# Pooled attention with a top-1 mixture of experts: part of the routing moves from VectorE to GpSimd and ScalarE, three weight pieces are split later, the row scatters lose their fillers

## The chip, the core and the metric

The kernel runs on one core of one Trainium2 chip. The core has five engines with queues of their own: TensorE (PE in the profile, with its weight loads as PEld), VectorE (DVE), ScalarE (ACT), GpSimd (POOL) and SyncE (SP), which here only issues DMA transfers. Each engine works through its queue in order; an instruction that waits holds up all behind it. The metric is the device time of one execution in microseconds, less is better.

## The reference

```python
def _attn_ref(q, k, v):                      # (8, 8, 576, 64) each
    k_p = k.reshape(B, H, 72, 8, D).mean(axis=3)
    v_p = v.reshape(B, H, 72, 8, D).mean(axis=3)
    scores = scale * np.matmul(q, k_p.transpose(0, 1, 3, 2))
    scores = scores - np.max(scores, axis=-1, keepdims=True)
    attn = np.exp(scores)
    attn = attn / (np.sum(attn, axis=-1, keepdims=True) + 1e-09)
    return np.matmul(attn, v_p)

def _moe_ref(x, w_gate, w1, w2):             # x: 4608 tokens of 512; 8 experts, 512 -> 1024 -> 512
    logits = x @ w_gate
    expert_idx = np.argmax(logits, axis=1)
    probs = softmax(logits)                  # maximum taken off, 1e-9 added to the sum
    gate_w = probs[np.arange(N), expert_idx]
    for e in range(E):                       # the rows of each expert
        h = np.maximum(x_sorted[lo:hi] @ w1[e], 0.0)
        y_sorted[lo:hi] = h @ w2[e]
    return gate_w[:, None] * y
```

## The kernel before, in words

**Attention.** The 4608 tokens are cut into 36 units of 128 (i = 0 to 35 in the loop at line 968). A unit's steps run over the engines in a fixed order: TensorE turns the queries (g_qt) and forms the scores two units ahead (g_s), VectorE takes the minimum (g_min), ScalarE the exponentials (g_exp); TensorE turns the probabilities (u_pt), ScalarE and VectorE write them as a high and a low half (u_pt's activation, "ph", and u_lo, "pl", line 519), TensorE multiplies them with the values (u_pv, lines 540 and 545) into one single PSUM tile `po`, and VectorE normalises (u_nrm: lines 577, 579, 581, 586, 588). The next unit's u_pv waits until lines 581 and 586 have emptied `po`.

**Keys and values.** GpSimd adds up groups of eight keys and values of each batch (pool_k, pool_v: lines 322 to 325, three large additions each). TensorE, ScalarE and VectorE turn and split them (prep); the last step, `low` (line 420), is on GpSimd, and behind it SyncE issues some 13 small copies of each batch into the masked tile vb (line 1002, at most four for a unit, `moves`). u_pv of that batch's units needs these copies.

**Routing.** The units are grouped by 6, 6, 6, 6, 6, 4 and 2 (groups 0 to 6). When a group's logits are there, `route` hands over a chain of some 18 small steps: maximum (`top`, 622), subtraction (`away`, 625), the choice of the expert (`best`, 631, `lowest`, `onehot`, 646), counting, ranks, the softmax sum (`total`) with its `guard` (679), and `gate`. They go into a list, `fillers`, and the unit loop takes one at each of about six fixed places of a unit (`fill`). `off` is true for groups 0 to 4: their steps `before_all`, `ident_ids`, `carry` and `spot_int` run on GpSimd. Behind group 2, `early_pe` to `early_shift` (720) note whether expert 0 has its first 256 rows.

**Scatters.** A group's rows are sent to the expert's place in DRAM by one indirect DMA for each unit (`scatter`, line 694, issued by GpSimd). They stand in the list `pend`; `flush(1)` takes one at the start of each unit, and a second one in the middle while more than two wait (line 997). The rows lie in a ring of 12 slots (XR); u_nrm of a unit writes the slot that a unit twelve before it had. Between two scatters with no larger GpSimd work between them, `apart` (line 599) puts two memsets of 128x512 as fillers, up to unit 29.

**Weights of expert 0.** Eight pieces are loaded (wload, line 100) into staging tiles and written as a high half (ScalarE, line 114, hooks at units 12 to 28) and a low half: pieces 0, 2, 5, 6, 7 on GpSimd (lines 122 and 123, at units 14, 20, 31, 26, 30), pieces 1, 3 and 4 on VectorE in quarters (`lsplit`, line 856) from the units that line 862 names.

**Around unit 30.** Behind unit 28's GpSimd work the tile xg is blanked (blank_x); in unit 29 SyncE loads the first 256 rows of expert 0 into it (early_load, line 906). At the start of unit 30 GpSimd's queue holds, in this order, the low half of weight piece 7, `first_block` (line 882 and following: it splits the loaded rows, so it waits for that load), one scatter, and then the steps that the chain of group 4 puts on GpSimd.

**Experts.** Behind the attention a loop of some 22 blocks of 256 rows runs the two layers of the experts on TensorE (lines 956 to 958 and 1027).

The places that the change touches:

Of the kernel before, what the change touches and what calls it, by code (L numbers as in the profile page):

```python
# [12 lines left out]
AF = mybir.ActivationFunctionType  # L13
OP = mybir.AluOpType
# [4 lines left out]
SX = 2.0 ** 6  # L19
SW = 2.0 ** 5  # L20
# [12 lines left out]
def kernel(  # L33
# [10 lines left out]
    nc = tc.nc  # L44
    B, H, S, D = q.shape
    N, Dm = out.shape
    E = w1.shape[0]
# [54 lines left out]
    last_pool = []  # L102
# [63 lines left out]
    zpad = consts.tile([128, XW], F32, name="zpad")  # L166
# [18 lines left out]
    tv = consts.tile([128, 1], F32, name="tv")  # L185
# [5 lines left out]
    okf = consts.tile([128, 1], F32, name="okf")  # L191
# [97 lines left out]
    KVS = {}  # L289
# [8 lines left out]
    def fill_pe():  # L298
        if fillers and fillers[0][1]:
            fillers.pop(0)[2]()  # L300
# [155 lines left out]
    def g_qt(G, j):  # L456
        b, r = units[groups[G][0]]
        pq = psA.tile([128, 512], F32, name="pq", bufs=2)
        for x in range(4):
            if r is None:  # L460
                src = ql[(b // 2) % 2][:, 2 * x:2 * x + 2, :].rearrange("p h d -> p (h d)")
            else:
                src = qt[b % 2][:, 4 * j + x, r:r + 2, :].rearrange("p r d -> p (r d)")
            nc.tensor.transpose(pq[:, x * 128:(x + 1) * 128], src, ident)
        if j == 0:
            QT[G] = work.tile([128, 8, 128], F32, name="qT", bufs=2)
        nc.scalar.activation(QT[G][:, 4 * j:4 * j + 4, :].rearrange("p h t -> p (h t)"), pq, AF.Copy)
# [4 lines left out]
    def g_s(G, j):  # L472
        b, r = units[groups[G][0]]
        ps = psA.tile([128, 512], F32, name="ps", bufs=2)
        t = QT[G]
        if r is None:
            for x in range(2 * j, 2 * j + 2):
                for s in range(2):
                    bd = BD[(b + s) % 3].rearrange("p s h x -> p (s h) x")
                    rhs = bd[:, 2 * x:2 * x + H + 2:H + 1, :]  # L480
                    nc.tensor.matmul(ps[64 * s:64 * s + 64, (x % 2) * 2 * KP:(x % 2 + 1) * 2 * KP],
                                     t[:, x, 64 * s:64 * s + 64], rhs, start=True, stop=True)
            slots = [(4 * j + x, 0) for x in range(4)]
        else:
            hs = range(2 * j, 2 * j + 2)
            for x, h in enumerate(hs):
                nc.tensor.matmul(ps[:, x * 2 * KP:(x + 1) * 2 * KP], t[:, h, :],  # L487
                                 BD[b % 3][:, :, h, :], start=True, stop=True)
            slots = [(h, s) for h in hs for s in range(2)]
        PS_[G, j] = (ps, slots)  # L490
        if j == stages(G) - 1:
            QT.pop(G)
# [7 lines left out]
    def g_exp(G, j):  # L500
        ps, nmx, slots = PS_.pop((G, j))
        for x, (h, s) in enumerate(slots):
            p = pbuf[groups[G][s] % 4]
            nc.scalar.activation(p[:, h * KP:(h + 1) * KP], ps[:, x * KP:(x + 1) * KP], AF.Exp,  # L504
                                 bias=nmx[:, x:x + 1], scale=-1.0)

    def u_pt(i):
        p = pbuf[i % 4]
        pp = psA.tile([128, 1024], F32, name="pp")
        for c in range(5):  # L510
            nc.tensor.transpose(pp[:, c * 128:(c + 1) * 128], p[:, c * 128:(c + 1) * 128], ident)
        ph = work.tile([128, 640], F16, name="ph")
        nc.scalar.activation(ph, pp[:, 0:640], AF.Copy, scale=SP)
        PP_[i] = (pp, ph)
# [76 lines left out]
    pend = []  # L591

    def flush(n=99, upto=99):
        while n and pend and pend[0][0] <= upto:
            _, f, u = pend.pop(0)
            f(u)
            n -= 1

    def apart():
        if last_pool and not KVS.get("late"):  # L600
            nc.gpsimd.memset(zpad[:, 0:Dm], 0.0)
            nc.gpsimd.memset(zpad[:, 0:Dm], 0.0)
        last_pool[:] = [1]

    EARLY = 3
# [1 line left out]
    def route(gidx):  # L607
        i0, gs = bounds[gidx]
        X, L = GRP.pop(gidx)
        L = L[:, 0:gs, :]  # L610
        sh = [128, gs, E]
        V = nc.vector
        off = gidx < len(bounds) - 2
        Z = {}

        def new(n, shape, dt=F32):
            Z[n] = work.tile(shape, dt, name="r" + n)
            return Z[n]
# [3 lines left out]
            V.tensor_reduce(m[:, :, 0], L, axis=AX.X, op=OP.max)  # L622

        def away():
            V.tensor_tensor(new("a", [128, 6, E])[:, 0:gs], L, Z["m"][:, 0:gs].to_broadcast(sh), op=OP.subtract)

        def soft():
            nc.scalar.activation(new("ex", [128, 6, E])[:, 0:gs], Z["a"][:, 0:gs], AF.Exp, scale=1.0 / SX)
# [47 lines left out]

        def guard():
            es = Z["es"][:, 0:gs]
            V.tensor_scalar(es, es, 1e-9, SX * SW * SW, op0=OP.add, op1=OP.mult)

        def spot_int():
            p = new("pos", [128, 6], I32)[:, 0:gs]
# [34 lines left out]
            V.tensor_copy(oki, okf[0:1, :])  # L717

        def early_shift():
            V.tensor_tensor(tv, tv, okf, op=OP.add)  # L720

        if gidx == len(bounds) - 1:
            return [top, away, best, lowest, before_all, onehot, count, carry], rank, \
                [ranked, spot, spot_int, total, ident_ids, guard, gate], soft, scatters
        chain = [before_all, top, away, best, lowest, onehot, soft, ident_ids, count, rank, carry, total, ranked, spot,
                 spot_int, guard, gate, scatters]
        if gidx == EARLY - 1:
            chain += [before_all, early_pe, early_int, early_shift, lambda: KVS.update(early=1)]
        for f in chain:
# [74 lines left out]
    def put(i, pos, f, *a):  # L804
        assert 0 <= i < NU
        hooks.setdefault((i, pos), []).append((f, a))
# [52 lines left out]
        put(at, "act2", wsplit, 0, j, "h")  # L859
    for j, at, what in ((0, 14, 'P'), (2, 20, 'P'), (5, 31, 'p'), (6, 26, 'p'), (7, 30, 'p')):  # L860
        put(at, "q", wsplit, 0, j, what)
    for j, at in ((1, 15), (3, 23), (4, 26)):
        for x in range(4):
            put(at + x, "dve" if x % 2 else "dve2", lsplit, j, x, 4)

# [61 lines left out]
    def run(i, pos):  # L927
        for f, a in hooks.pop((i, pos), []):
            f(*a)
# [38 lines left out]
    for i in range(NU):  # L968
        A, Z = halves.get(2 * i), halves.get(2 * i + 1)
        Y = halves.get(2 * i - 1)  # L970
        run(i, "q")
        flush(1)
        if i:
            u_pt(i)
        if A:
            g_s(*A)
        if Y:
            g_exp(*Y)
        if i in turns:
            g_qt(*turns[i])  # L980
        if (i, "pe") not in hooks:
            fill_pe()
        run(i, "pe")
        if i:
            u_lo(i)
        fill()
        if A:
            g_min(*A)
            fill()
            g_exp(*A)  # L990
        run(i, "act")
        run(i, "dve")
        u_pv(i)
        run(i, "pe2")
        if i == 29:
            KVS["late"] = 1
        if len(pend) > 2:
            flush(1)
        fill_pe()
        run(i, "sp")  # L1000
        for _ in range(min(4 if i < 30 else 8, len(moves))):
            nc.sync.dma_start(*moves.pop(0))
        if Z:
            g_s(*Z)
        u_nrm(i, (lambda: g_min(*Z)) if Z else None)
        run(i, "act2")
        run(i, "dve2")
        last = routes(i)
        fill(2 if i >= NU - 3 else 1)
# [3 lines left out]
    front, rank, back, soft, scatters = last  # L1013
    V = nc.vector
# [288 lines left out]
```

## Time and profile before

| | us |
|---|---|
| median of 3 runs | 648.05 |
| the runs | 646.21, 648.05, 651.86 |
| profiled execution, its own time | 650.54 |
| its span | 648.10 |

| engine | busy us | share of the span |
|---|---|---|
| PE | 585.6 | 90% |
| DVE | 329.9 | 51% |
| ACT | 286.2 | 44% |
| POOL | 275.6 | 43% |

The shares are means over two stages that differ. The attention fills the first third of the span, the expert loop the rest. In the attention no engine is busy all the time: what sets its length is which engine waits for which, unit by unit. An idle time in brackets behind an instruction is how long its engine had nothing to do before it, with what ended that wait. The clock is what the throttle granted TensorE: 1.00 stands for 2.4 GHz, 0.50 for 1.2 GHz.

### The profile page before, as it was taken

To read this page: it belongs to the slowest core of one execution; us is meant where nothing else is said; L and a number is where in the kernel's file an instruction comes from. 1 tells how busy PE (TensorE), PEld (TensorE's weight loads), DVE (VectorE), ACT (ScalarE), POOL (GpSimd) and SP (SyncE) were. 2 spreads that over 40 slices of the span, in tenths; PEclk is the share of its full clock that TensorE was granted. 3 is DMA by queue.
4 is the path that set the end of the run, shared out by engine and by line. 5 is a ranking of instruction groups with operands and counts; after the bars stand their busy time and mean duration, and the time that the engine had idled before them with its cause. 6 is when DMAs were issued, how large, how long until landed. Compare 5 with 4: busy or idle time off the path is not lost. (4 is left out here: it accounts for less than half of the span.)

```text
span 648.1 us, 15925 instructions
## 1 busy us (share of the span) xinstructions
PE 585.6 (90%) x4694; PEld 430.1 (66%) x4695; DVE 329.9 (51%) x683; ACT 286.2 (44%) x630; POOL 275.6 (43%) x531
## 2 busy tenths in 40 slices
PE   6698888798789878998899999999999989999995
PEld 6587777797768454675466677666667656677663
DVE  6568976988777417212764655213732262220212
ACT  1565775687663126221763644223622352221222
POOL 5796599898696532212215033212131232112212
PEclk9898997998889979999899999999999979999999
DMA  8994679964748673973479397633222323213200
GB/s 234 304 302 137 210 230 241 302 205 151 229 115 303 221 132 77 378 235 82 120 245 337 92 320 225 205 81 89 40 62 68 92 68 97 49 49 81 65 16 30
DMA packets 104203, 105.61 MB, mean 163 GB/s; under 512 B 62310, under 2 KB 72550, under 8 KB 104168
## 3 DMA queue, kind: packets, MB, share of 16 engines
q1 hardware_dynamic: 97528, 85.46, 47.0%
q0 software_dynamic: 6640, 19.71, 8.2%
q8 instruction: 19, 0.31, 0.2%
q14 instruction: 16, 0.13, 0.1%
HBM read 71.77 MB, written 22.06 MB: 145 GB/s over the span
## 5 line engine op out<-in xcount | busy, mean ns | idle before, releaser
L1027 PEld LDWEIGHTS <-bd 128*128 128x128 f16 x936 | 91.3, 98 | 105.7 <-ACT bd L1017 1.0
L1212 POOL TENSOR_TENSOR spacer<-ql,iG 1x1 f32<-1x1 f32 x44 | 23.8, 540 | 220.7 <-ACT ql L1208 219.7
L1021 DVE SCALAR_TENSOR_TENSOR bd<-ps,bd 128x512 f16<-128x512 f32 x44 | 30.1, 689 | 152.2 <-ACT bd L1017 152.2
L504 ACT ACTIVATE both<-ps,nmx 128x72 f32<-128x72 f32 x288 | 68.7, 326 | 29.5 <-DVE nmx L497 28.8
L1021 DVE SCALAR_TENSOR_TENSOR bd<-pp,bd 128x512 f16<-128x512 f32 x44 | 30.3, 690 | 100.6 <-ACT bd L1017 100.6
L1017 ACT ACTIVATE bd<-pp 128x512 f16<-128x512 f32 x44 | 26.2, 597 | 108.9 <-PE pp L958 78.8
L1017 ACT ACTIVATE bd<-ps 128x512 f16<-128x512 f32 x44 | 26.1, 597 | 77.3 <-PE L956 67.9
L487 PE MATMUL ps<-bd,qT 128*128 128x144 f32 x256 | 49.6, 322 | 11.2 <-ACT both L504 5.5
L1027 PE MATMUL po<-kv,bd 128*128 128x512 f16 x264 | 58.8, 379 | 0.0
L1027 PE MATMUL po<-w,bd 128*128 128x512 f16 x264 | 58.8, 379 | 0.0
L1213 POOL DMA_INDIRECT out_dram<-ql,iG x44 | 43.8, 995 | 21.8 <-issue 20.2
L956 PE MATMUL ps<-kv,w 128*128 128x256 f16 (+1 forms) x176 | 44.8, 268 | 8.5 <-DMA kv<-bd 5.6
L956 PE MATMUL ps<-kv,qt 128*128 128x256 f16 (+1 forms) x176 | 46.1, 270 | 4.5 <-issue 3.0
L1027 PE MATMUL pq<-kv,bd 128*128 128x512 f16 x216 | 48.1, 379 | 0.0
L487 PEld LDWEIGHTS ps<-bd,qT 128*128 128x128 f32 x256 | 39.1, 210 | 13.0 <-ACT both L504 8.4
L958 PE MATMUL ps<-kv,qt 128*128 128x256 f16 (+1 forms) x176 | 46.2, 270 | 1.6 <-DVE qt L116 1.6
L545 PE MATMUL po<-vb,ph 128*128 128x146 f16 (+2 forms) x384 | 34.3, 237 | 14.8 <-DVE l L586 6.6
L958 PE MATMUL ps<-kv,w 128*128 128x256 f16 (+1 forms) x176 | 44.9, 268 | 2.6 <-DVE w L116 2.6
L957 PE MATMUL ps<-kv,qt 128*128 128x256 f16 (+1 forms) x176 | 46.2, 270 | 0.0
L957 PE MATMUL ps<-kv,w 128*128 128x256 f16 (+1 forms) x176 | 44.9, 268 | 0.0
L956 PE MATMUL pp<-kv,qt 128*128 128x256 f16 (+1 forms) x176 | 44.7, 263 | 0.0
L957 PE MATMUL pp<-kv,qt 128*128 128x256 f16 (+1 forms) x176 | 44.7, 263 | 0.0
(235 smaller groups left out, 1369.2 us busy)
## 6 DMA issues: line engine op xcount, KB each, us to landing
both<-in_moe_w_dram SPq DMA_DIRECT2D x6, 2048.0 KB, 11.5
st<-in_moe_w_dram SPq DMA_DIRECT2D x6, 2048.0 KB, 13.6
vb<-x_by_expert SPq DMA_DIRECT2D x17, 514.0 KB
st<-in_moe_w_dram SPq DMA_DIRECT2D x8, 1024.0 KB
kv<-in_k_dram SPq DMA_DIRECT2D x7, 1024.0 KB
kv<-in_v_dram SPq DMA_DIRECT2D x7, 1024.0 KB
qt<-in_q_dram SPq DMA_DIRECT2D x6, 1024.0 KB
qt<-in_q_dram SPq DMA_DIRECT2D x4, 512.0 KB
```

Of the source, the lines that this page charges most:

```text
L487: nc.tensor.matmul(ps[:, x * 2 * KP:(x + 1) * 2 * KP], t[:, h, :], BD[b % 3][:, :, h, :], start=True, stop=True)
L504: nc.scalar.activation(p[:, h * KP:(h + 1) * KP], ps[:, x * KP:(x + 1) * KP], AF.Exp, bias=nmx[:, x:x + 1], scale=-1.0)
L545: nc.tensor.matmul(po[:, half, cols], a[:, c * 128:(c + 1) * 128], VB[b % 3][:, y, c, sl, 0:CW], start=st, stop=False, skip_group_check=True)
L956: nc.tensor.matmul(dst, wh, xT[:, d, 0:n], start=(d == 0), stop=False)
L957: nc.tensor.matmul(dst, wh, xT[:, DC + d, 0:n], start=False, stop=False)
L958: nc.tensor.matmul(dst, wl, xT[:, d, 0:n], start=False, stop=(d == DC - 1))
L1017: nc.scalar.activation(hT[0][:, 2 * k:2 * k + 2, :].rearrange("p f t -> p (f t)"), pH[k], AF.Relu)
L1021: V.scalar_tensor_tensor(l, pH[k], 0.0, h, op0=OP.max, op1=OP.subtract)
L1027: nc.tensor.matmul(y, hT[x][:, f, 128 * j:128 * j + 128], W2[s][z][:, f, :], start=(half == x == z == f == 0), stop=(half == z == 1 and f ...
L1212: nc.gpsimd.tensor_tensor(spacer[:, 0:1], ys[j][0:1, 0:1], iG[0:1, j:j + 1].bitcast(F32), op=OP.add)
L1213: st = nc.gpsimd.indirect_dma_start(out=out, out_offset=bass.IndirectOffsetOnAxis(ap=iG[:, j:j + 1], axis=0), in_=ys[j], in_offset=None, b ...
```

## The change

Six things change. The subtraction `away` of groups 0 to 4 runs on GpSimd. Their `guard` runs on ScalarE, as one activation that scales and adds. `early_shift` runs on GpSimd. In the chain, `ident_ids` stands right behind `away`, and `guard` ahead of `spot`. The quarters of the low halves of weight pieces 1, 3 and 4 start at units 24, 25 and 28 in place of 15, 23 and 26. The two memsets of `apart` go, and up to unit 28 a second scatter in a unit is issued only when more than six wait, not more than two.

```diff
--- before.py
+++ after.py
@@ -597,9 +597,6 @@
             n -= 1
 
     def apart():
-        if last_pool and not KVS.get("late"):
-            nc.gpsimd.memset(zpad[:, 0:Dm], 0.0)
-            nc.gpsimd.memset(zpad[:, 0:Dm], 0.0)
         last_pool[:] = [1]
 
     EARLY = 3
@@ -622,7 +619,8 @@
             V.tensor_reduce(m[:, :, 0], L, axis=AX.X, op=OP.max)
 
         def away():
-            V.tensor_tensor(new("a", [128, 6, E])[:, 0:gs], L, Z["m"][:, 0:gs].to_broadcast(sh), op=OP.subtract)
+            (nc.gpsimd if off else V).tensor_tensor(new("a", [128, 6, E])[:, 0:gs], L,
+                                                    Z["m"][:, 0:gs].to_broadcast(sh), op=OP.subtract)
 
         def soft():
             nc.scalar.activation(new("ex", [128, 6, E])[:, 0:gs], Z["a"][:, 0:gs], AF.Exp, scale=1.0 / SX)
@@ -676,7 +674,10 @@
 
         def guard():
             es = Z["es"][:, 0:gs]
-            V.tensor_scalar(es, es, 1e-9, SX * SW * SW, op0=OP.add, op1=OP.mult)
+            if off:
+                nc.scalar.activation(es, es, AF.Copy, scale=SX * SW * SW, bias=1e-9 * SX * SW * SW)
+            else:
+                V.tensor_scalar(es, es, 1e-9, SX * SW * SW, op0=OP.add, op1=OP.mult)
 
         def spot_int():
             p = new("pos", [128, 6], I32)[:, 0:gs]
@@ -717,13 +718,13 @@
             V.tensor_copy(oki, okf[0:1, :])
 
         def early_shift():
-            V.tensor_tensor(tv, tv, okf, op=OP.add)
+            nc.gpsimd.tensor_tensor(tv, tv, okf, op=OP.add)
 
         if gidx == len(bounds) - 1:
             return [top, away, best, lowest, before_all, onehot, count, carry], rank, \
                 [ranked, spot, spot_int, total, ident_ids, guard, gate], soft, scatters
-        chain = [before_all, top, away, best, lowest, onehot, soft, ident_ids, count, rank, carry, total, ranked, spot,
-                 spot_int, guard, gate, scatters]
+        chain = [before_all, top, away, ident_ids, best, lowest, onehot, soft, count, rank, carry, total, ranked, guard,
+                 spot, spot_int, gate, scatters]
         if gidx == EARLY - 1:
             chain += [before_all, early_pe, early_int, early_shift, lambda: KVS.update(early=1)]
         for f in chain:
@@ -859,7 +860,7 @@
         put(at, "act2", wsplit, 0, j, "h")
     for j, at, what in ((0, 14, 'P'), (2, 20, 'P'), (5, 31, 'p'), (6, 26, 'p'), (7, 30, 'p')):
         put(at, "q", wsplit, 0, j, what)
-    for j, at in ((1, 15), (3, 23), (4, 26)):
+    for j, at in ((1, 24), (3, 25), (4, 28)):
         for x in range(4):
             put(at + x, "dve" if x % 2 else "dve2", lsplit, j, x, 4)
 
@@ -994,7 +995,7 @@
         run(i, "pe2")
         if i == 29:
             KVS["late"] = 1
-        if len(pend) > 2:
+        if len(pend) > (2 if i >= 29 else 6):
             flush(1)
         fill_pe()
         run(i, "sp")
```

## Rows read from the trace of the kernel before

**Rows 1.** Busy us by stretch: PE, PEld, DVE, ACT, POOL; clock, DMA share.

```profile
90.00:120.00 30.00, 25.55 (x255) 22.50 (x255) 23.37 (x65) 21.09 (x69) 27.32 (x33) 0.89 0.92 261
...
235.00:640.00 405.00, 393.42 (x2889) 263.03 (x2886) 157.17 (x182) 151.06 (x202) 95.54 (x268) 0.99 0.45 130
```

**Rows 2.** Groups on DVE, 60 to 210 us: busy us, mean ns.

```profile
L856 DVE SCALAR_TENSOR_TENSOR w<-st,w 128x256 f16<-128x256 f32 x12 | 11.1, 922 | 1.9 <-ACT w L114 1.9
...
L679 DVE TENSOR_SCALAR res<-res 128x6 f32<-128x6 f32 (+1 forms) x6 | 5.1, 843 | 0.0
L625 DVE TENSOR_TENSOR ra<-L,rm 128x48 f32<-128x48 f32 (+2 forms) x7 | 4.9, 698 | 0.0
L720 DVE TENSOR_TENSOR tv<-tv,okf 128x1 f32<-128x1 f32 x1 | 3.5, 3549 | 0.0
```

**Rows 3.** Line 856 alone: ns shortest/median/longest, first and last start.

```profile
L856 DVE SCALAR_TENSOR_TENSOR w<-st,w x12: 406/415/3283, 113.4 to 180.0; 128x256 f16<-128x256 f32 x12
```

**Rows 4.** Groups of instructions of POOL, 60 to 210 us.

```profile
L601 POOL MEMSET zpad<- 128x512 f32 x10 | 5.4, 541 | 0.0
...
L420 POOL TENSOR_TENSOR vc<-u,vc 128x40 f16<-128x40 f32 x6 | 1.6, 266 | 10.3 <-DVE vc L417 8.2 <-DVE ri L577 2.0
```

**Rows 5.** TensorE at three of its stalls: start, us, [idle before].

```profile
100.23 0.96 PE L545 MATMUL po<-vb,ph 128*128 128x73 f16 x7 [0.69 <-DMA vb<-vc]
...
126.27 0.66 PE L545 MATMUL po<-vb,pl 128*128 128x146 f16 x6 [2.23 <-DVE pl L519]
...
149.47 0.71 PE L545 MATMUL po<-vb,ph 128*128 128x146 f16 x8 [2.87 <-DVE l L586]
```

**Rows 6.** Busy time in the 4 us behind the second stall of rows 5.

```profile
128.00:132.00 4.00, 4.00 (x37) 3.98 (x36) 3.59 (x14) 3.29 (x11) 3.08 (x6) 0.75 0.93 316
```

**Rows 7.** DVE in order of time (start us, us, line, operation [idle before]).

```profile
66.20 1.62 DVE L625 TENSOR_TENSOR ra<-L,rm 128x48 f32<-128x48 f32 x1
...
68.85 0.62 DVE L631 SCALAR_TENSOR_TENSOR req<-ra,down 128x48 f32<-128x48 f32 x1
...
122.19 3.28 DVE L856 SCALAR_TENSOR_TENSOR w<-st,w 128x256 f16<-128x256 f32 x1
...
183.47 1.65 DVE L625 TENSOR_TENSOR ra<-L,rm 128x48 f32<-128x48 f32 x1
...
185.52 0.68 DVE L581 TENSOR_TENSOR both<-po,ri 128x512 f32<-128x512 f32 x1
...
191.11 0.17 DVE L577 TENSOR_SCALAR ri<-po 128x8 f32<-128x8 f32 x1 [2.44 <-PE po L545]
```

**Rows 8.** GpSimd in order of time, first half of the attention.

```profile
64.85 2.91 POOL L322 TENSOR_TENSOR st<-kv 128x1280 f32<-128x1280 f32 x1
...
80.43 1.21 POOL L694 DMA_INDIRECT x_by_expert<-both,rpos  x1 [1.74 <-DVE ri L577]
...
85.35 0.28 POOL L420 TENSOR_TENSOR vc<-u,vc 128x40 f16<-128x40 f32 x1
```

**Rows 9.** GpSimd in order of time, second half of the attention.

```profile
128.38 0.25 POOL L420 TENSOR_TENSOR vc<-u,vc 128x40 f16<-128x40 f32 x1 [2.01 <-DVE ri L577]
...
149.40 0.28 POOL L420 TENSOR_TENSOR vc<-u,vc 128x40 f16<-128x40 f32 x1
...
185.29 1.89 POOL L882 TENSOR_TENSOR bd<-vb,zf 128x1024 f16<-128x1024 f32 x1 [0.24 <-DMA vb<-x_by_expert]
...
190.69 1.01 POOL L694 DMA_INDIRECT x_by_expert<-both,rpos  x1 [0.16 <-issue]
```

**Rows 10.** ScalarE in order of time, the high part of weight piece 4.

```profile
168.56 1.06 ACT L114 ACTIVATE w<-st 128x1024 f16<-128x1024 f32 x1 [2.04 <-DMA st<-in_moe_w_dram]
```

**Rows 11.** SyncE's queue in order of time: when it issues transfers.

```profile
85.65 3.94 SPq L1002 DMA_DIRECT2D vb<-vc  x4
...
158.07 0.52 SPq L100 DMA_DIRECT2D st<-in_moe_w_dram  x1
...
180.28 0.37 SPq L906 DMA_DIRECT2D vb<-x_by_expert  x1
```

## The prediction

> **What bounds the kernel now.** First the stretches [rows 1]. In the expert loop TensorE works 393 of 405 us, and the change leaves that loop alone; what it gives or takes lies in the attention. There no engine is full (between 90 and 120 us TensorE works 25.6 of 30 us), but GpSimd is near it with 27.3. So the length is a matter of waits. Second, VectorE's groups [rows 2, 3]: one and the same instruction, a quarter of a weight piece, takes 0.41 us or up to 3.28. The long ones end with a GpSimd addition that began before them: `away` at 66.20 ends at 67.82, GpSimd's addition at 67.76 [rows 7, 8]. Third, TensorE's stalls [rows 5], three kinds. At 100.23 it waits for the small copies of vb. At 126.27 it waits 2.23 us for "pl", which stands behind a quarter that began at 122.19 and took 3.28 [rows 7]. At 149.47 it waits 2.87 us for line 586, behind `early_shift` with its 3.55 us [rows 2]. A stall costs more than itself: after the second one the granted clock is 0.75 over 4 us [rows 6], some 1 us of lost work. Fourth, the copies and loads that SyncE issues [rows 11]: they start when GpSimd's `low` is done [rows 8, 9], and TensorE or ScalarE wait at their ends [rows 5, 10].
>
> **The change part by part.**
>
> *Memsets of the scatters.* Ten pairs, two times 0.54 us each [rows 4]: 10.8 us off GpSimd, none off VectorE directly. What this is worth is counted below, where a `low` is late.
>
> *Second scatters.* No scatter goes away. Up to unit 28 each unit issues one, so the scatters of a group come one to three units later; of group 3, three (not one) are left for the places behind `first_block`. A ring slot is then written some two units behind the issue of the scatter that reads it. A transfer takes about 5.0 us from issue to use (the early load, 180.28 to 185.29) [rows 9, 11], two units near 8 to 10: 0 to 3 us of wait in units 22 to 25. I take 0, because these units have a wait at their end that covers it (step 2).
>
> *`guard` on ScalarE.* Six took 5.1 us [rows 2]; five move, 4 to 5 us off VectorE. On ScalarE I take 0.25 us each, the nearest small operation [rows 4], between 0 and the 1.06 of a 1024-wide activation [rows 10]. ScalarE waits there for TensorE anyway, and `total` is two places earlier. Behind it on ScalarE stands the next unit's "ph". Path: 0 to minus 1 each; 0 taken, as the unit ends on copies or loads.
>
> *`early_shift` on GpSimd.* 3.55 us off VectorE, 0.27 on GpSimd [rows 2, 4]; TensorE's wait of 2.87 at 149.47 goes. Whether the end sees it, step 2 says.
>
> *Quarters moved.* Twelve at a mean of 0.92 and a median of 0.415 [rows 2, 3]: 6.1 us are blocking. In units 15 to 18 they go. In units 24 to 31 they come back as 0.41 each, two in some units; units 27 and 28 get one more each, and unit 27's `low` comes behind one: 0.4 us.
>
> *`away` on GpSimd.* Five of seven [rows 2] leave VectorE; GpSimd needs 0.27 each (the 128x40 subtraction, rows 4; no less than 0.2, no more than twice that). This adds a wait: `best` on VectorE now waits for GpSimd's queue, and behind `best` stand line 581, the minimum, line 586 and the next "pl", for which TensorE waits. In group 0 nothing is won: GpSimd's 2.91 us addition (now behind `ids`) starts at some 66.6 and holds `best` until 69.5, where `away` and `best` ended before [rows 7, 8]. In groups 1 to 3 GpSimd has by then no backlog, since the memsets and a scatter are gone.
>
> The Trainium skill, "SBUF — State Buffer", section "Who interferes with whom", says that a VectorE instruction with two SBUF inputs contends with a GpSimd one that reads SBUF, and that the first holds the port for its whole length. `best` at 68.85 (0.62 us) agrees [rows 7]. By that rule alone moving `away` only hands the block to `best`, and the five would save 0; by the row of line 625 they would save some 3 us.
>
> **The sum, in three steps.** *Step 1, copies of batch 3.* `low` runs at 85.35, long after VectorE is ready. Ahead of it GpSimd waited for and issued a scatter, 78.69 to 81.64 [rows 8]. That scatter now comes a unit later: 2.95 us less, but `spot` stands one place later, about 1 us (line 581 with 0.68, rows 7, and a minimum). So `low`, the copies at 85.65 [rows 11] and the stall that ends at 100.23 [rows 5] come 1.9 us earlier (0 to 2.95).
>
> *Step 2, units 15 to 27.* The quarter at 122.19 costs 2.87 us of blocking and the clock behind it: 3.5. The first quarter, at 113.4 [rows 3], I put at 1.2, a third of the other blocking (6.1 less 2.87). With step 1, unit 18 is 6.6 earlier (3 to 8). From there GpSimd sets the pace: from `low` at 128.38 to `low` at 149.40 it works 21.0 us [rows 9]; a memset pair of 1.1 goes, a scatter of 1.0 with its 0.2 us gap enters, and small gaps close: 0.4 less. That second `low` starts SyncE's chain to the load at 158.07 [rows 11], whose end ScalarE awaits at 168.56, 2.04 us [rows 10]. Unit 27 so begins 7.0 earlier. The 2.87 of `early_shift`, the blocked guard and what is left of the quarters would bring TensorE there another 5 us earlier; it waits instead.
>
> *Step 3, unit 30.* GpSimd's queue holds the low half of piece 7, `first_block`, a scatter, then `away` of group 4. `first_block` starts when the early load has landed, 185.29 [rows 9]; that load follows `low` and four copies on SyncE, so saved memsets don't bring it nearer. The scatter ends at 191.70 [rows 9], `away` at some 191.95. Before, VectorE began it at 183.47 [rows 7] and line 581 followed at 185.52; now `best` holds line 581 until 192.2, 6.7 us later. Before, TensorE waited there for copies, and unit 31 reached line 577 at 191.11 [rows 7]. Now its product starts at some 193.5 and "pl" follows two operations that the split of piece 5 can block: 196.5 to 198.5, 6.6 later (5.4 to 7.4).
>
> Minus 1.9, minus 4.7, minus 0.4, plus 0.4, plus 6.6: **0.0 us** against the profiled span of 648.10. That execution took 650.54, 2.5 over the median of the three, so I set the change of 0 on the median: 648.
>
> **The rivals.**
>
> *A: group 4's wait is short, the rest is kept (0.24).* The load of the first rows lands earlier, or copies cover VectorE's stall as they cover TensorE's now (until 191.11, rows 7). Then the 6.6 shrink to 0 to 2: 641 to 643. If also the weight load comes earlier and the 2.87 of `early_shift` and the clock behind it count, 4 more: 637. For it: three batches of copies, all late for GpSimd's sake. Against it: one queue, in order, and 185.29 waits for a DMA.
>
> *B: the gains stop at fixed chains, the loss stays (0.18).* If copies and the load at 158.07 are bound by SyncE and the transfers themselves, `low` being earlier brings nothing, every gain before unit 27 ends in a longer wait there, and step 3 stands alone: plus 6.6 and 0.4, 655. It decides from the point where `low` of batch 3 (85.35) and of batch 6 (149.40) are not at least 1 us earlier against the units around them [rows 8, 9]. For it: DMA share 0.92 between 90 and 120 us [rows 1]. Against it: the gap between `low` and the first copy is 0.02 us [rows 8, 11].
>
> *C: the block follows (0.08).* A VectorE operation that begins beside a long GpSimd addition ends with it, as at 66.20 and 122.19 [rows 7, 8]. The moved quarters land beside the splits of pieces 5, 6 and 7 and beside `first_block`. Three more blocks of up to 1.9 us, the length of such a GpSimd operation [rows 9], outside the covered units would add 5: 653. The rule of the Trainium skill's page "SBUF — State Buffer", section "Who interferes with whom", is the same thing said in general.
>
> **How the numbers follow.** Within 1% (6.5 us, about what can be told from no change) lies the forecast, 0.50, by itself 643 to 653 from the bounds of the steps, and most of C. A gives most of the faster side, B the slower. Faster 0.25, same 0.55, slower 0.20. For 8 in 10 the range takes in A without its farthest end and B with some of the ring's 3 us: 640 to 657.
>
> **What would show it.** Right: unit 30 has a VectorE wait of 6 to 8 us ahead of `best` (line 631), released by GpSimd's subtraction behind `first_block`; ScalarE's wait before the high part of piece 4 grows from 2 to some 6; the stalls at 126 and 149 are gone; the copies of batch 3 start near 83.8. Wrong: no such wait in unit 30 (then A); equal starts of the copies (B); waits of line 581 for the scatters' transfers, or of `best` in groups 1 to 3, which I have at 0.

## The result and the profile after

The changed kernel takes **656.58 us** (median of 4 runs, 656.10 to 656.89) beside 647.13 of the kernel before (4 runs, 643.59 to 651.86): ratio **1.0119, 95% interval 1.0076 to 1.0162**. It is slower by some 1.2%; the forecast was no change. The profiled execution took 656.1, its span is 653.7, which is 5.6 over the span of before. The ratios leave out a kernel's runs that are over 1.5% above its fastest; since the runs of one kernel on one chip spread by up to 2.7%, this takes more runs from a kernel with many of them (13 of the 35 of the kernel before beside e1 to e4, one of the 12 of each of those) and can raise a ratio, so the medians of all runs stand beside it in the table of the experiments.

VectorE's groups in the kernel after, attention and experts together (busy us, mean ns | idle us ahead, what ended it):

```profile
L857 DVE SCALAR_TENSOR_TENSOR w<-st,w 128x256 f16<-128x256 f32 x12 | 9.2, 764 | 0.0
...
L629 DVE SCALAR_TENSOR_TENSOR req<-ra,down 128x48 f32<-128x48 f32 x5 | 6.2, 1232 | 6.3 <-POOL ra L622 6.3
```

The quarters fell only from 922 to 764 ns [rows 2]. The five subtractions are gone from VectorE, but the operation behind them, `best`, takes 1.23 us each, and waits 6.3 us in all for GpSimd (2.10 in group 2, 0.79 in group 3, 3.41 in group 4). Before, these five `best` took 0.29 each:

```profile
L625 DVE TENSOR_TENSOR ra<-L,rm 128x48 f32<-128x48 f32 x5 | 4.5, 906 | 0.0
...
L631 DVE SCALAR_TENSOR_TENSOR req<-ra,down 128x48 f32<-128x48 f32 x5 | 1.4, 286 | 0.0
```

So 4.5 us left VectorE, 4.8 came back as longer `best`, and 6.3 of waiting came on top. The two operations that moved as expected were the guard (five on ScalarE, 0.21 us each) and `early_shift` (0.19 us on GpSimd, 3.55 before).

TensorE's stalls after (start, us, [idle ahead and what ended it]):

```profile
124.01 0.24 PE L545 MATMUL po<-vb,ph 128*128 128x146 f16 x1 [2.10 <-DMA vb<-vc]
...
132.27 0.95 PE L545 MATMUL po<-vb,ph 128*128 128x146 f16 x12 [2.14 <-DVE rm L634]
...
170.40 1.65 PE L545 MATMUL po<-vb,ph 128*128 128x146 f16 x12 [3.51 <-ACT ph L513]
...
182.87 0.64 PE L545 MATMUL po<-vb,pl 128*128 128x146 f16 x6 [2.10 <-DVE pl L519]
...
195.41 1.72 PE L545 MATMUL po<-vb,ph 128*128 128x146 f16 x12 [5.04 <-issue]
```

The stall for "pl" at 126.27 [rows 5] has become one for the copies of the next batch, at 124.01; the one at 149.47 is gone; three new ones stand ahead of the products of units 19, 29 and 31. Line 577 marks the end of a unit's product on VectorE. Against the kernel before it comes 1.5 us earlier in units 17 and 18, 1.7 **later** in unit 19, 0.7 later in 27, 3.9 later in 29 and 7.4 later in 31 (198.52 beside 191.11 [rows 7]). Of that, 7.1 is left at the last unit of the attention and 5.6 in the span.

GpSimd after, in order of time:

```profile
85.34 0.27 POOL L420 TENSOR_TENSOR vc<-u,vc 128x40 f16<-128x40 f32 x1
...
124.74 2.89 POOL L322 TENSOR_TENSOR st<-kv 128x1280 f32<-128x1280 f32 x1 [6.66 <-DMA kv<-in_k_dram]
...
128.83 0.28 POOL L622 TENSOR_TENSOR ra<-L,rm 128x48 f32<-128x48 f32 x1
...
150.47 0.27 POOL L420 TENSOR_TENSOR vc<-u,vc 128x40 f16<-128x40 f32 x1
...
185.43 1.90 POOL L883 TENSOR_TENSOR bd<-vb,zf 128x1024 f16<-128x1024 f32 x1 [1.36 <-DMA vb<-x_by_expert]
...
190.82 1.01 POOL L695 DMA_INDIRECT x_by_expert<-both,rpos  x1 [0.15 <-issue]
191.86 0.28 POOL L622 TENSOR_TENSOR ra<-L,rm 128x48 f32<-128x48 f32 x1
192.25 1.89 POOL L122 TENSOR_TENSOR kv<-st,swc 128x1024 f32<-128x1024 f32 x1
```

Here the forecast can be read against the trace row by row. `low` of batch 3 stands at 85.34, before 85.35 [rows 8]; `low` of batch 6 at 150.47, before 149.40 [rows 9]. Both were to come earlier, by 1.9 and 7.0. In between stands the reason: GpSimd is through with its shorter queue at 118.08 and then waits 6.66 us for a load. The subtraction of group 2 stands behind that addition and a scatter: it runs at 128.83. The subtraction of group 4 comes out of the queue at 191.86 and ends at 192.14 (the forecast said 191.95), behind `first_block` and a scatter.

The same addition in the kernel before, and SyncE's queue there, which holds its next load until the values that the addition reads have landed (its wait, then its issue, then GpSimd):

```profile
SPq L244 <- DMA kv<-in_v_dram: 3.4, 1, 3.4
...
122.05 0.37 SPq L244 DMA_DIRECT2D kv<-in_k_dram  x1
...
122.30 2.89 POOL L322 TENSOR_TENSOR st<-kv 128x1280 f32<-128x1280 f32 x1
```

There GpSimd came to this addition at 122.30 without any wait, 0.25 us behind SyncE's release. The two were level: what is taken from GpSimd ahead of this point becomes a wait, unless the load comes earlier too.

VectorE after, in unit 18 and then from unit 29 to unit 31:

```profile
129.14 1.89 DVE L629 SCALAR_TENSOR_TENSOR req<-ra,down 128x48 f32<-128x48 f32 x1 [2.10 <-POOL ra L622]
...
179.72 2.36 DVE L857 SCALAR_TENSOR_TENSOR w<-st,w 128x256 f16<-128x256 f32 x1
...
192.18 2.04 DVE L629 SCALAR_TENSOR_TENSOR req<-ra,down 128x48 f32<-128x48 f32 x1 [3.41 <-POOL ra L622]
194.14 0.68 DVE L581 TENSOR_TENSOR both<-po,ri 128x512 f32<-128x512 f32 x1
...
198.52 0.17 DVE L577 TENSOR_SCALAR ri<-po 128x8 f32<-128x8 f32 x1 [0.17 <-PE po L545]
```

`best` waits until 192.18, and then ends at 194.22, beside GpSimd's addition of line 122, which runs from 192.25 to 194.14. Line 581, which empties the tile that TensorE waits for, starts at 194.14 (before 185.52 [rows 7]). In unit 18 the same happens to group 2, which the forecast had at 0: `best` waits 2.10 us for the subtraction, takes 1.89, line 581 comes behind it, and TensorE stalls at 132.27. There the 1.6 us by which unit 18 was earlier become the 1.7 by which unit 19 is later.

### The profile page after: what moved, and what is told of

The parts are those of the page before. It is cut to its first block, busy times and chain, and to the rows that moved or that the text cites. A ratio compares the mean times of both kernels' runs of the same rounds, so it can differ in the third digit from the quotient of the medians.

```text
span 653.7 us, 15904 instructions
## 1 busy us (share of the span) xinstructions
PE 584.7 (89%) x4694; PEld 430.8 (66%) x4695; DVE 324.6 (50%) x672; ACT 287.1 (44%) x635; POOL 268.2 (41%) x517
## 5 line engine op out<-in xcount | busy, mean ns | idle before, releaser
L1214 POOL DMA_INDIRECT out_dram<-ql,iG x44 | 43.7, 993 | 21.4 <-issue 20.2
L957 PE MATMUL ps<-kv,qt 128*128 128x256 f16 (+1 forms) x176 | 47.4, 275 | 4.9 <-issue 3.5
L957 PE MATMUL ps<-kv,w 128*128 128x256 f16 (+1 forms) x176 | 43.8, 262 | 7.3 <-DMA kv<-bd 4.5
L487 PEld LDWEIGHTS ps<-bd,qT 128*128 128x128 f32 x256 | 39.3, 211 | 14.8 <-ACT both L504 6.9
L959 PE MATMUL ps<-kv,qt 128*128 128x256 f16 (+1 forms) x176 | 47.5, 275 | 1.7 <-DVE qt L116 1.7
L958 PE MATMUL ps<-kv,qt 128*128 128x256 f16 (+1 forms) x176 | 47.5, 275 | 0.0
L959 PE MATMUL ps<-kv,w 128*128 128x256 f16 (+1 forms) x176 | 43.9, 263 | 2.6 <-DVE w L116 2.6
L545 PEld LDWEIGHTS <-ph 128*128 128x128 f16 x384 | 28.1, 103 | 25.8 <-issue 13.8
```

Of the source, the lines that this page charges most:

```text
L545: nc.tensor.matmul(po[:, half, cols], a[:, c * 128:(c + 1) * 128], VB[b % 3][:, y, c, sl, 0:CW], start=st, stop=False, skip_group_check=True)
L957: nc.tensor.matmul(dst, wh, xT[:, d, 0:n], start=(d == 0), stop=False)
L958: nc.tensor.matmul(dst, wh, xT[:, DC + d, 0:n], start=False, stop=False)
L959: nc.tensor.matmul(dst, wl, xT[:, d, 0:n], start=False, stop=(d == DC - 1))
L1214: st = nc.gpsimd.indirect_dma_start(out=out, out_offset=bass.IndirectOffsetOnAxis(ap=iG[:, j:j + 1], axis=0), in_=ys[j], in_offset=None, b ...
```

## The experiments

Eighteen kernels on five chips (e1 to e4, e5 to e8, e9 to e12, e13 to e16, e17 and e18), each beside runs of the kernel before on its chip. The changed kernel itself was run beside the kernel before alone. "28 to 31" is the time from line 577 of unit 28 to that of unit 31 in the profiled execution (before 14.5, after 20.7); e18, whose profiled execution was one of its longest, is left out there and of all groups of profiles below.

| kernel | median us (before beside it) | ratio, 95% interval | ratio of medians | 28 to 31 |
|---|---|---|---|---|
| e1 | 647.52 (647.30) | 1.0045, 1.0004 to 1.0085 | 1.000 | 14.2 |
| e2 | 647.97 (647.30) | 1.0036, 0.9993 to 1.0078 | 1.001 | 18.7 |
| e3 | 647.85 (647.30) | 1.0054, 1.0015 to 1.0094 | 1.001 | 17.5 |
| e4 | 645.26 (647.30) | 1.0012, 0.9971 to 1.0053 | 0.997 | 15.2 |
| e5 | 656.47 (658.85) | 0.9975, 0.9943 to 1.0007 | 0.996 | 15.3 |
| e6 | 664.99 (658.85) | 1.0076, 1.0036 to 1.0116 | 1.009 | 15.1 |
| e7 | 663.65 (658.85) | 1.0090, 1.0061 to 1.0120 | 1.007 | 21.9 |
| e8 | 659.26 (658.85) | 1.0011, 0.9982 to 1.0041 | 1.001 | 15.5 |
| e9 | 644.48 (648.98) | 0.9931, 0.9904 to 0.9959 | 0.993 | 14.9 |
| e10 | 647.57 (648.98) | 1.0000, 0.9973 to 1.0027 | 0.998 | 17.5 |
| e11 | 645.42 (648.98) | 0.9959, 0.9929 to 0.9989 | 0.995 | 14.7 |
| e12 | 644.35 (648.98) | 0.9927, 0.9892 to 0.9961 | 0.993 | 14.2 |
| e13 | 649.01 (650.25) | 1.0012, 0.9972 to 1.0052 | 0.998 | 14.2 |
| e14 | 650.07 (650.25) | 0.9995, 0.9949 to 1.0041 | 1.000 | 15.0 |
| e15 | 651.75 (650.25) | 1.0052, 1.0012 to 1.0092 | 1.002 | 20.5 |
| e16 | 648.42 (650.25) | 0.9981, 0.9946 to 1.0015 | 0.997 | 14.8 |
| e17 | 646.26 (648.27) | 0.9975, 0.9935 to 1.0015 | 0.997 | 14.0 |
| e18 | 649.40 (648.27) | 0.9974, 0.9930 to 1.0019 | 1.002 | |

**The subtraction of group 4.** e1 is the changed kernel with

```
-  (nc.gpsimd if off else V).tensor_tensor(new("a", ...
+  (nc.gpsimd if (off and gidx < 4) else V).tensor_tensor(new("a", ...
```

> The changed kernel, but the subtraction of group 4 back on VectorE; groups 0 to 3 stay on GpSimd. Theory 1 (a wait behind first_block): in the changed kernel unit 31 lost 4.1 us against before (191.11 to 198.52, 3.3 us late one unit earlier), with a wait of 3.41 us for the subtraction and a block of 1.8 us behind it. Without it some 4 us come back: 652.5, 0.8% over before. Theory 2 (the moved quarters are blocked by the splits of the weight pieces in units 28 to 31, and that is the loss): the wait goes but the quarters stay, and no more than 1 us comes back: 655.5 or more.

e2 is the changed kernel with all subtractions on V.

> The changed kernel with the subtraction of all groups back on VectorE; the guard on ScalarE, the order of the chain, the quarters and the scatters stay changed. Theory 1: what groups 0 to 3 lose or win ends in the wait for copies and loads before unit 27, so the time is that of the run with group 4 alone put back, 652.5 within 1 us. Rival: the waits of 2.1 us and the block of 1.7 us at group 2 (unit 18) and 0.8 us at group 3 are on the path; then it is 3 to 4 us below that run, 649.

e7 is the kernel before with `(nc.gpsimd if gidx == 4 else V)` in that line, e8 the same with `gidx < 4`.

> The kernel before with nothing changed but that the subtraction of group 4 runs on GpSimd. Theory 1 (it waits behind first_block): VectorE waits for it 6 to 7 us in unit 30, TensorE loses what the copies of batch 7 do not cover anyway: unit 31 comes 4 to 6 us later, 652 to 653. Rival (the loss needs the fewer memsets and the later quarters and scatters of the changed kernel): 647 to 648.

> The kernel before with nothing changed but that the subtraction of groups 0 to 3 runs on GpSimd. GpSimd is behind VectorE around units 12 and 18 here, since memsets and second scatters are still in its queue, so the choice of the expert waits for it: 1 to 2 us each at groups 1 and 2. Theory of fixed chains: these end in the wait for the load at unit 27, 647 to 648. If they reach the end: 649 to 651. If the port was what cost: 645.

e15 is the changed kernel with the quarters' units of before, `((1, 15), (3, 23), (4, 26))`.

> The changed kernel with one part undone: the quarters of pieces 1, 3 and 4 are back in units 15, 23 and 26; the subtraction of group 4 stays on GpSimd. If the prices of the quarters (1.1%, e9 against e1) and of group 4 (0.7%, e1 against the changed kernel) add up, the ratio is 0.998 to 1.003. If the wait behind first_block takes back whatever is gained before it, the ratio is 1.005 to 1.012. As in the forecast, with quarters that save time where they are moved to, it would be above the changed kernel: 1.015 or more.

One operation is the main price. Put back, it takes 1.0119 to 1.0045 (e1; more than the 4 us expected); done alone, it makes the kernel before slower by 0.9% (e7, 5.9 us; 4.8 by the medians). Groups 0 to 3 cost and give nothing in time (e8; e1 and e2 are equal within their intervals); but `best` of group 2 has no wait in e8, whose GpSimd keeps its memsets and comes no earlier to the load, and e2 loses 4.5 us more than e1 between units 28 and 31, so neither shows what the wait in unit 18 costs by itself. VectorE in e7, unit 30:

```profile
189.74 1.89 DVE L632 SCALAR_TENSOR_TENSOR req<-ra,down 128x48 f32<-128x48 f32 x1 [8.53 <-POOL ra L625]
191.78 0.69 DVE L581 TENSOR_TENSOR both<-po,ri 128x512 f32<-128x512 f32 x1
```

and GpSimd in e7, which runs the subtraction behind `first_block` and a scatter, and the next piece behind it:

```profile
188.38 1.01 POOL L695 DMA_INDIRECT x_by_expert<-both,rpos  x1 [0.16 <-issue]
189.42 0.28 POOL L625 TENSOR_TENSOR ra<-L,rm 128x48 f32<-128x48 f32 x1
189.66 1.90 POOL L122 TENSOR_TENSOR kv<-st,swc 128x1024 f32<-128x1024 f32 x1
```

The three kernels that have it on GpSimd (after, e7, e15) take 20.5 to 21.9 us from unit 28 to unit 31; the other sixteen, with the kernel before, take 14.0 to 18.7, on average 15.3 against 21.0. The difference of 5.7 us agrees with e7's 5.9 (a mean over kernels that differ in other parts too). e15 came out at the lower end of its second case, with an interval (and a ratio of medians) that holds the first as well: with the quarters back the changed kernel is still 0.2 to 0.5% above the kernel before.

**The quarters.** e3 is the kernel before with the new units alone:

```
-    for j, at in ((1, 15), (3, 23), (4, 26)):
+    for j, at in ((1, 24), (3, 25), (4, 28)):
```

> The kernel before with nothing but the quarters of weight pieces 1, 3 and 4 moved to units 24, 25 and 28. Step 2 of the forecast: the block of 2.87 us at unit 18 and the one at unit 16 go and reach the end, minus 4.7: 642 to 643. Theory of fixed chains: unit 18 is then held by the copies of batch 4 and by the load of batch 6's values, and unit 27 by the weight load, so nothing is won there, and the quarters in units 28 to 31 cost 0 to 2.5: 647 to 650.

e9 is e1 with the old units; e13 moves piece 1 alone, e14 piece 4 alone. e17 and e18 are all of the change without its subtractions, with the quarters in the old units and in the new (e18 is e2 again, beside its partner).

> The changed kernel with the subtraction of group 4 on VectorE and the quarters of pieces 1, 3 and 4 in their old units 15, 23 and 26; all its other parts stay. If the moved quarters are what keeps e1 0.45% above the kernel before (a quarter of piece 4 beside the split of piece 7, 2.4 us in unit 29), the ratio falls to 0.998 to 1.001 and no quarter in units 28 to 31 takes over 1.5 us. If the quarters are free because other waits cover them, the ratio stays at e1's 1.0045.

> The kernel of e9 with the quarters of piece 1 in units 24 to 27 in place of 15 to 18 (pieces 3 and 4 stay in 23 and 26). If it is the move of piece 1 that costs (five more quarters beside those of pieces 3 and 4 in units 24 to 27), the ratio rises from 0.993 to 0.999 to 1.004. If the price lies in units 28 to 31, where piece 4 goes, it stays at 0.991 to 0.996.

> The kernel of e9 with the quarters of piece 4 in units 28 to 31 in place of 26 to 29 (pieces 1 and 3 stay in 15 and 23). If the block of a quarter beside the split of piece 7 and first_block is the price, the ratio rises from 0.993 to 0.997 to 1.003; if piece 1 is the price, it stays at 0.991 to 0.996.

> The kernel before with scatters without memsets and held back, guard on ScalarE, the new order and early_shift on GpSimd; all subtractions on VectorE, the quarters in their old units 15, 23 and 26. If these parts save what e9 showed: 0.991 to 0.996, and 0.5 to 1.1% below e18. If e9 owed its 0.9931 to its chip and the quarters are free: 0.998 to 1.003, equal to e18 within 0.4%.

> The kernel of e17 with the quarters of pieces 1, 3 and 4 in units 24, 25 and 28, as in the changed kernel (this is the kernel of e2 beside its partner on one chip). If the moved quarters cost: 1.001 to 1.006, 0.5 to 1.1% above e17. If they are free: equal to e17 within 0.4%. As the forecast had it (quarters moved save 4.7 us): 0.7% below e17.

None of the kernels with all three moved (after, e1, e2, e3, e18) is measurably faster than its partner with the old units, so the forecast's 4.7 us don't reach the end. Whether the move costs something stays open: by the ratios e3 is 0.5% above the kernel before (0.1% by the medians) and e1 1.1% above e9 (two chips), but e18 equals e17 on one chip, 0.5% apart in their medians, which their intervals don't resolve. e9 came out below both of its cases, and e13 and e14 each where its own piece would be the price; but e16 on their chip and e17 on another, with the old units, lie above e9 too. e17 and e18 came out near e17's second case: not as low as e9, and level with each other.

The profiles tell more of the gain. From line 577 of unit 13 to that of unit 17, five kernels with piece 1 moved (after, e1, e2, e3, e13) take 15.0 to 17.8 us, mean 16.3; nine without (before, e4, e7, e8, e9, e14 to e17) 17.6 to 19.3, mean 18.5. So 2.2 us are gained there. From unit 17 to unit 19 the same five take 14.2 on average and the nine 11.4, but the quarters are not what takes this back: e2 and e3, whose subtractions are all on VectorE, take 12.4 and 12.3 (TensorE waits 2.0 and 1.9 us for copies). The 14.5 to 15.9 stand in after, e1, e13 and, with piece 1 in its old units, e14: the four profiles in which `best` of group 2 waits (1.4 to 2.7 us) and then takes 1.9. Whether it waits is not the program's doing alone. e9, e14 and e15 run the same program up to unit 25 and take 9.9, 14.5 and 10.4 from unit 17 to unit 19; GpSimd had awaited the load 3.4, 5.8 and 2.8 us. So a difference of one or two us between two single profiles proves little.

In e3 the gain is still there at unit 27 (67.0 us from unit 13; before 70.2, and 68.9 in e7, the same program up to there) and is lost between units 28 and 31 (17.5, before 14.5). A moved quarter of piece 4 stands there beside the split of piece 5 and holds line 577 of unit 31:

```profile
188.34 2.91 DVE L856 SCALAR_TENSOR_TENSOR w<-st,w 128x256 f16<-128x256 f32 x1
191.18 0.15 DVE L577 TENSOR_SCALAR ri<-po 128x8 f32<-128x8 f32 x1
```

e10 has the same quarter with the same 2.91 us and the same 17.5; e2 takes 18.7. e1 and e14, with piece 4 moved as well, take about as long there as e9 with the old units (14.2 and 15.0, beside 14.9).

**GpSimd's saved work.** e4 is the kernel before without the two memsets and with the second scatter held back; e16 is e4 with `early_shift` on GpSimd:

```
-            nc.gpsimd.memset(zpad[:, 0:Dm], 0.0)
-            nc.gpsimd.memset(zpad[:, 0:Dm], 0.0)
...
-        if len(pend) > 2:
+        if len(pend) > (2 if i >= 29 else 6):
```

> The kernel before without the memsets and with the second scatter of a unit held back up to unit 28; nothing else. Step 1 of the forecast: the last step of batch 3 on GpSimd comes 2 to 3 us earlier and with it the stall of unit 13: 645. Theory of fixed chains: the copies start earlier, but the end is set by later loads: 647 within 1 us. If the three scatters left for unit 30 to 32 cost something: 648 to 649.

> The kernel before with two edits: scatters without memsets and held back, and early_shift on GpSimd. Theory that early_shift's 2.87 us at TensorE and GpSimd's memsets carry the gain of e9 and e12: 0.992 to 0.996. Theory of the forecast, that unit 27's wait for the load of piece 4 swallows them: 0.998 to 1.002, as e4 with the scatters alone (1.001).

Neither differs measurably from the kernel before; e16 lies where the forecast's theory has it. The wait for the load behind 118 us, in e4:

```profile
122.67 2.90 POOL L322 TENSOR_TENSOR st<-kv 128x1280 f32<-128x1280 f32 x1 [2.60 <-DMA kv<-in_v_dram]
```

Where the memsets are gone GpSimd is ready for this addition 30 to 32 us behind line 577 of unit 10; where they are kept, 36 to 38: some 6 us saved (e6, whose copies are moved, is left aside here). All thirteen such kernels then wait, 1.1 to 6.7 us, 3.8 on average; of the five that keep the memsets (before, e3, e7, e8, e10) four don't wait at all and one 0.7. So the addition itself starts only 2.4 us earlier on average, which is by how much units 10 to 13 have become shorter. From `low` of batch 4 to `low` of batch 5, the stretch that holds this load, the thirteen take 31.2 us on average (29.3 to 34.3) and the five 31.4: there the saved work is all wait.

**The loads and copies.** e5 is e2 with the high parts of pieces 4, 5 and 7 one unit later, e6 is e2 with eight copies a unit in place of four:

```
-    for j, at in enumerate((12, 13, 18, 17, 26, 27, 23, 28)):
+    for j, at in enumerate((12, 13, 18, 17, 27, 28, 23, 29)):
```
```
-        for _ in range(min(4 if i < 30 else 8, len(moves))):
+        for _ in range(min(8, len(moves))):
```

> The run without the subtraction on GpSimd (e2), and the high parts of weight pieces 4, 5 and 7 on ScalarE one unit later (27, 28, 29 in place of 26, 27, 28). Theory of fixed chains: in e2 TensorE waits 4.41 us at unit 27 because ScalarE waits for the load of piece 4 ahead of the probabilities. One unit later, some 4 us, that load has nearly landed; the wait at unit 27 falls to 0 to 1 and the unit comes 3 to 4 us earlier. What of this reaches unit 31 is limited by the next chain, the copies of batch 7 behind unit 27; those start earlier too, so 3 us reach the end: 644 to 645. Rival (the copies of batch 6, issued ahead of that load, are as late as the load): the wait only changes its name, 647 to 648.

> The run without the subtraction on GpSimd (e2), and SyncE may issue eight of the small copies in a unit, not four, so that a batch's copies stand together in its queue, ahead of the loads that stood between them. Theory of fixed chains: the waits for copies at unit 18 (1.98 us in e2) and at units 22 and 31 shrink, as the copies end 1 to 3 us earlier; the loads behind them come that much later, and the wait for the load of piece 4 at unit 27 grows. Units 18 to 22 come 2 us earlier, the end 0 to 2: 645 to 648. Rival (the copies are slow because the DMA engines are full, not because of their place in the queue): unit 18 does not move, 648.

e10, e11 and e12 put the later high parts (with the quarters of piece 4 at 28) on the kernel before, on e9 and on e16.

> The kernel before with one edit: the high parts of pieces 4, 5 and 7 on ScalarE in units 27, 28 and 29 in place of 26, 27 and 28, and the quarters of piece 4 two units later (28), since they need the high part. Theory that unit 27 is held by the load of piece 4: ScalarE's 2.04 us wait there goes and TensorE's wait after it, ratio 0.996 to 0.998. Rival, that GpSimd's queue sets units 19 to 27 by itself: the wait returns in another form in the same units and the ratio is 1.000; with the block of a quarter of piece 4 beside the split of piece 7 up to 1.003.

> The kernel of e9 (scatters without memsets and held back, guard on ScalarE, early_shift and groups 0 to 3 of the subtraction on GpSimd, quarters of pieces 1 and 3 in their old units) with the high parts of pieces 4, 5 and 7 one unit later and the quarters of piece 4 at 28. Theory that the parts of the change save time which the load of piece 4 takes back at unit 27: ratio 0.990 to 0.995. Rival, that a later load (piece 5 or 7, for the same queue) takes the place of the one that is gone: 0.998 to 1.001, with a wait of ScalarE of 3 us or more in units 28 to 33.

> The kernel before with three edits: scatters without memsets and held back, early_shift on GpSimd, and the high parts of pieces 4, 5 and 7 one unit later (quarters of piece 4 at 28). Guard, order and subtraction stay as they were. If the 2.87 us of early_shift and the memsets reach the end once the wait for the load of piece 4 is gone: ratio 0.991 to 0.995, as low as e11 or lower. If guard and order carry the gain of e11: 0.997 to 1.000, above e11. If nothing reaches the end: 1.000 for both.

e6 shows SyncE's order at work. With the copies ahead of the loads it lost 0.8%: the wait for copies at unit 18 (1.98 in e2) went, as expected, but TensorE waited much longer for them at unit 13,

```profile
100.71 1.14 PE L545 MATMUL po<-vb,ph 128*128 128x219 f16 x8 [6.30 <-DMA vb<-vc]
```

and GpSimd's addition started at 126.55, the latest of all, after 5.07 us of wait. The later high parts do take ScalarE's wait for the load of piece 4 away (2.04 before [rows 10], 4.39 after, none in e5 and e10), and yet e10 is at 1.000 and e11 no lower than e9, its partner on the same chip. In e5 the gain of 7.1 us at unit 27 (164.99 beside 172.13) is spent by unit 33, where TensorE stalls 5.51 us; but that says nothing of the change. VectorE and ScalarE wait there for something that the trace calls remote and doesn't name (5.75 and 7.28 us), and such waits stand in the profiles of all four kernels on that chip (e5 to e8) and in none of the others.

So unit 27's wait for the load is not what caps the gains; e10 loses them in units 28 to 31, and why e11 is no lower than e9 is not shown.

**A version faster than both kernels**: e12 (0.9927), e9 (0.9931) and e11 (0.9959) on one chip, 0.4 to 0.7% faster than the kernel before, with intervals below 1; e12 lies in the range of its first theory, e11 just above it. Their nearest relatives on other chips, e16 and e17, are at 0.998 with intervals that hold 1. So what is left of the change without the two parts (e9, e17) is worth between nothing and 0.7%.

## Why the prediction was wrong

- **Step 1 acted, and less than forecast** (copies of batch 3, minus 1.9). From `low` of batch 2 to `low` of batch 3 the kernel before takes 20.87 us and the one after 19.53 (65.81 to 85.34); the five kernels with the memsets take 20.9 to 21.4, the thirteen without 18.2 to 19.5, the lower end where the order of the steps stays (e4, e12, e16), so that the place which `spot` loses costs some 1.1, as the step had it. The 1.3 us are there, 1.9 were forecast. In the profiled execution `low` of batch 2 was itself 1.3 late (65.81 against 64.48), so that copies and `low` stood where they had been [rows 8, 11]; unit 13 came 0.9 earlier.
- **Step 2 failed** (units 15 to 27, minus 4.7 and minus 0.4). Unit 18 was to come 6.6 earlier and came 1.6; unit 27 was to begin 7.0 earlier and came 0.7 later. The blocking of piece 1's quarters was real: 2.2 us are gained between units 13 and 17 (0.6 in the changed kernel's own profile). The 0.4 less from `low` to `low` was right for kernels without memsets in which group 2 doesn't wait (20.5 or 20.6 in e2, e4, e9, e15, e16 and e17, 21.0 before [rows 9]); the quarter of unit 27, forecast at 0.4, doesn't show in e2, and the 21.4 after belong to the profiles in which `best` of group 2 waited (21.3 to 21.4 in e1, e13 and e14). What failed is "From there GpSimd sets the pace" and, with it, the 0 for "`best` in groups 1 to 3", taken since "GpSimd has by then no backlog". The load that GpSimd awaits behind 118 us sets the pace: GpSimd, earlier by its shorter queue, waited 6.66 us for it, and the subtraction of group 2, now in that queue, came behind it, so that `best` waited 2.10 us and TensorE 2.14. That turned unit 18's 1.6 earlier into unit 19's 1.7 later. No such wait stood in the kernel before, since GpSimd and the load were level there. The forecast had fixed chains as rival B, with the point from which it decides (`low` of batches 3 and 6 not 1 us earlier), and gave it 0.18 because SyncE followed `low` by 0.02 us. That gap told who is released by whom at one place; it said nothing of who is late at the next. B's 655 lies near the result partly by luck, since its loss was to be step 3's alone.
- **Step 3 was right in place and mechanism**: `best` waits behind `first_block` and a scatter, the subtraction ends at 192.14 (forecast 191.95), line 581 starts behind it. Its size was put at 6.6; unit 31 lost 4.1 against unit 30 (10.15 beside 6.07), e7 puts the price at 5.9 and the stretches at 5.7. The VectorE wait was 3.4, not 6 to 8, since VectorE came to it at 188.77 (192.18 less 3.41), 5.3 us behind the 183.47 of before [rows 7]; `best` itself then took 2.04 us, which the step had not counted.
- **Rival C was right as a mechanism** and under-rated. The quarter at 179.72 took 2.36 beside the first addition of piece 7's split, and unit 29 lost 2.65 (3.93 less 1.28). The move of the quarters is not the cause of this block: with the old units e9 and e15 have the block too, while the kernel before had its quarter at 179.97, 1 us ahead of that addition. GpSimd reached that addition 4.35 us behind line 577 of unit 28 there, and 1.8 to 2.2 behind it in after, e4, e9, e15 and e16: without the memsets GpSimd is earlier, and so the quarter meets it. Where the moved quarters do land beside a split, as the rival said, is unit 31 of e3 and e10.
- **`away` of groups 0 to 3** was put at some 3 us of VectorE's time for all five, 0 by the rule of the Trainium skill ("SBUF — State Buffer", section "Who interferes with whom"). The trace agrees with the rule: the five `best` grew by 4.8, the five `away` had taken 4.5, and e8 is at 1.001. The waits of `best`, 2.9 us in groups 2 and 3, are a price of their own, for which the forecast had 0.
- The ring of slots (0 to 3 us, 0 taken) shows no wait; the guard on ScalarE costs 0.21 us each and releases nothing that the end sees.
- Some numbers of the forecast don't follow from its own rows: 2.87 and "some 1 us" of clock make 3.9, not 3.5; a third of 6.1 less 2.87 is 1.1, not 1.2; the middle of 5.4 to 7.4 is 6.4, not 6.6. None of them decides. And the quarter at 122.19 began 0.11 us ahead of GpSimd's addition (122.30), not behind it.

In one line: minus 1.9, minus 4.7 and minus 0.4 came out as plus 0.7 at unit 27 (with the plus 0.4 of the quarters), and plus 6.6 as plus 6.7 from unit 27 to unit 31, of which 4.1 are the step's own and 2.6 the block. The forecast's zero was a sum of a loss that exists and of gains that were used up before unit 27.

## What to carry to other kernels

A gain ahead of a point at which two chains are level is worth only what the other chain gains too: before counting it, look for the next load or copy that the engine doesn't wait for today only because it is late itself, and check whether that transfer moves too. A loss needs no such cover, so of a forecast that nets gains against a loss, trust the loss first. A small operation moved into an in-order queue costs the whole queue that is ahead of it, with the loads that this queue waits for (groups 2 and 4 here), and the step that follows it on the old engine inherits the contention that the moved one had.

## What the runs showed of the hardware

A VectorE operation on 48 elements took 2.04 us (192.18 to 194.22) beside a GpSimd addition that began at 192.25, 0.07 us later by the trace; it ended with the addition (194.14), though it is recorded as the first of the two. In e3 a quarter was recorded 0.72 us ahead of such an addition (188.34 and 189.06), took 2.91 us where others took 0.41, and ended 0.3 us behind it. And the level differs between chips: the kernel before took 647.3, 658.85, 648.98, 650.25 and 648.27 us on five of them, 1.8% apart, with runs from 638.4 to 653.6 on one chip, so kernels on different chips are compared by their ratios to the kernel before alone. The slowest of the five is the one whose four profiles (e5 to e8) have the waits called remote, of up to 12.6 us; no other profile has one.
